# One core, attention and a gated convolution in one kernel: the list of 1,028 steps in a new sequence

## The chip, the cores and the metric

The kernel runs on one core of a Trainium2 chip. The metric is the device time of one execution in microseconds (us), lower is better; the time given for a kernel is the median of its runs. One core has five engines that take their own instruction queues: PE (TensorE, the matmuls), DVE (VectorE), ACT (ScalarE), POOL (GpSimd) and SP (SyncE, which here only issues DMA transfers). They meet only at semaphores: an instruction waits until what it reads has been written and what it overwrites has been read.

## The reference

Four batches of eight attention heads over 768 positions, and behind them a projection, a circular convolution along the positions with a given filter, a product of three terms and a second projection:

```python
def _attn_ref(q, k, v, is_retrieval, n_sink, window):      # 4 x 8 heads x 768 x 64
    scores = scale * np.matmul(q, k.transpose(0, 1, 3, 2))
    stream_keep = causal & (is_sink | in_win)              # 4 sinks, window of 64
    mask = np.where(retr, full_mask, stream_mask)          # heads 0, 2 and 6 see all before them
    ...                                                    # softmax along the keys
    return np.matmul(a, v)

def _moe_ref(x, w_proj, filter_fft, w_out):                # x: 4 x 768 x 512
    proj = x @ w_proj
    x1, x2, x3 = proj[..., :D], proj[..., D:2 * D], proj[..., 2 * D:]
    X2 = np.fft.rfft(x2, n=S, axis=1)
    H = np.fft.rfft(filter_fft, n=S, axis=0)
    x2_conv = np.fft.irfft(X2 * H, n=S, axis=1)
    return (x1 * x2_conv * x3) @ w_out
```

Inputs and output are float32; the kernel computes in bfloat16 with float32 sums.

## The kernel before

The heads are taken in 16 pairs, n = 0 to 15; pair n belongs to batch b = n // 4. The work is cut into 1,028 named steps in its main part. Each is a small function, and the program is two strings of names that `run` goes through: `AHEAD` (start-up, not touched) and then `FAST`. No scheduler stands behind them: the sequence of the names is the sequence of the instructions on each engine's queue. So a step earlier in the string is earlier on its engine, and the engines run against each other as their waits allow.

```python
def run(words):
    for word in words.split():
        name, _, slot = word.partition("@")     # @n: the PSUM bank from which the step's tile begins
        name, _, eng = name.partition("/")      # /v: DVE, /s: ACT, /p: POOL
        now.update(slot=slot, engine=eng)
        ops[name]()
```

A name without a letter has a fixed engine. A copying step (`ev`, L969) goes to DVE (L971), POOL (L973) or ACT (L975); a step of two operands (`two`, L978) to DVE or POOL. The eight PSUM banks are the tile `space`.

The steps of a pair n:

- `lq`, `lk`, `lv`: load q, k, v (SP, DMA). `cq`, `ck`, `cv`: cast them to bfloat16 (L971, L973 or L975).
- `T`: turn q and k, for n below 8 on PE with `E` taking them out of PSUM, from 8 on as a DMA transpose issued by SP.
- `kx`, `ks`, `vx`, `vs`: copies of keys and values that the windowed heads need.
- `sc n.c`: scores (PE, L1452), `sb` (PE, L1465, n below 4) adds the mask, `ex` the exponential (ACT, L1471) into `f_pT`; `mk`, `mr` (L978) multiply by a mask for n from 4 on.
- `at`: probabilities by values (PE, L1516), `rec` (DVE, L1522) the reciprocals of the sums, `nm` the division into `f_attn`: one DVE instruction (L1533), or, with /s, twelve ACT instructions (L1530).
- `fd`, `fe`, `fA`, `fS`, `fb` (L978) and `fr` (DVE): sums and differences ahead of the forward transform, `W` the transform itself (PE), `We` its copy into `f_xh`.
- `tn`, `te`: the attention's result turned, into `f_xT` (for n up to 7 and 15 on PE, else as a DMA transpose).

The steps of a batch b:

- `X b.t.u`: the projection x2 in the frequency domain (PE, L1620), t one of three parts of the spectrum; `Xe` copies it into `f_X`; `sw` swaps halves of part 2 by DMA; `pa`, `pb`, `pc` (L978) multiply by the filter `f_HAB` into `r_P`.
- `x1 b.cb.s`, `x3 b.cb.s`: the projections x1 and x3 (PE, L1655) of one fourth of the channels, cb; `xs` copies x1; `g` (DVE, L1674, and L1678 for cb = 3) multiplies by x3 into `r_gy`.
- `c b.cb.r`: the inverse transform (PE, L1685) from `r_P`, `ce` its copy, `cv b.cb.half` (DVE, L1696) into `f_conv`; `y` (L978) multiplies by `f_conv`. For cb = 3, `y` comes ahead of `g`: `y` multiplies `f_conv` by x1 and `g` then by x3; else `g` comes first.
- `o b.i.part`: the output projection (PE, L1712) from `r_gy`; `oe` copies it out of PSUM, `st` stores it (SP, DMA).

Once only: `lw part.half` (POOL, L1244) loads w_proj in six pieces into `f_wproj`, part 0 for x1, 1 for x2, 2 for x3; `lwo` w_out, `lfilt` the filter; `fold`, `F` and `H` (L1272 on DVE, L1274 on ACT) make `f_HAB` of the filter, with `Hd0`, `Hd1` as DMAs; `G`, `Gt`, `Ge`, `Gk` make the transforms' tables; `blank` steps are matmuls on zeros.

The PE's dependence on the others at the places that the change touches: in the new list `X2.0.0` uses the banks that `nm12` reads; in the old one `x12.1.1` comes behind `X2.0.0` and uses banks that `g1.3` reads; `c2.0.0` needs all three of `pc2.0`, `pc2.1` and `pc2.2`; `tn7` needs `nm7`.

Of the kernel before, what the change touches and what calls it, by code (L numbers as in the profile page):

```python
# [146 lines left out]
ex7.0 X0.1.0@2 rec5 mk6.1/p nm5/v X0.1.1 Xe0.0/s mk7.0/v sc7.1@0 fd5/v Xe0.1/s sc6.2@4 fe5/v X0.2.0@6 pa0.0/v
ex7.1 pb0.1/v X0.2.1 ck8/v ex6.2 x30.1.0@2 pa0.1/v Xe0.2/s fA5/v sc7.2@0 ck10/v W4.1@4 cq8/s x30.1.1 mk7.1/v
sw0.0 sw0.1 mr6/v ex7.2 sc6.4@6 W4.0 T8 mk6.2/v ck9/s g0.1 mk7.2/p tn5@0 tn4@1 cq10/s te5/v x30.2.1@2 te4/v
cv7/s T10 x30.2.0 fS5/v pc0.1/v We4/s x10.2.0@0 fb5/v vs7/v ex6.4 x10.2.1 pa0.2/v lq11 cq9/s vx7/v at6.0@4 fr5  # L150
cv8/s T9 pb0.2/v at6.1 xs0.2/s W5.1@6 W5.0 pc0.2/v We5/s lv11 g0.2 pb0.0/p c0.0.0@0 cv9/s c0.1.0@1 lk13 rec6
# [1681 lines left out]
```

## Time and profile before

| | |
|---|---|
| runs | 195.18, 195.27, 194.32 us, median 195.18 |
| profiled execution | 194.51 us, of it the span of the instructions 192.7 |
| granted TensorE clock | 0.997 |
| PE busy | 177.3 us (92%), 1688 matmuls |
| DVE busy | 166.4 us (86%), 322 instructions |
| ACT busy | 141.4 us (73%), 202 instructions |
| POOL busy | 74.2 us (39%), 106 instructions |
| DMA | 34.25 MB, mean 178 GB/s |

The profile names instructions by their line, engine, operation and tiles (out<-in). A row of the groups gives busy us, mean ns of one, the engine's idle time ahead of them and what ended it. A row of the timeline gives start and duration in us, and in brackets how long the engine had waited and for what. Since many steps share a line (L978 above all), a single step is told by its tiles and its place in time.

### The profile page before, as it was taken

What the parts mean: (1) busy time and instruction counts of PE and PEld (TensorE: products, weight loads), DVE (VectorE), ACT (ScalarE), POOL (GpSimd) and SP (SyncE); (2) the same over time, 40 slices, a digit from 0 to 9 for tenths busy, and PEclk for the clock granted to TensorE, in tenths of its full rate; (3) what the DMA queues carried; (4) which work ended last, traced back from release to release, by engine and by line L of the source; (5) the groups of instructions that cost most, each with busy time, mean ns of one, the idle gap of its engine ahead of it and who ended that gap; (6) DMA issues with size and microseconds to landing.
All of it is one profiled execution on the core that took longest, in us unless ns stands there. A gap on an engine that the chain in (4) does not pass through costs nothing.

```text
span 192.7 us, 4452 instructions
## 1 busy us (share of the span) xinstructions
PE 177.3 (92%) x1688; PEld 102.5 (53%) x1688; DVE 166.4 (86%) x322; ACT 141.4 (73%) x202; POOL 74.2 (39%) x106
## 2 busy tenths in 40 slices
...
GB/s 161 324 268 301 199 197 242 270 297 222 189 217 198 235 198 182 227 221 209 232 165 218 271 251 207 164 58 41 0 155 109 43 110 0 26 31 23 273 263 112
DMA packets 79759, 34.25 MB, mean 178 GB/s; under 512 B 69106, under 2 KB 76018, under 8 KB 79730
## 3 DMA queue, kind: packets, MB, share of 16 engines
...
## 4 chain that ended last, share of the span: by engine, by line
PE 41%; DVE 27%; DMA 16%; ACT 8%; issue 4%; SPq 1%; POOL 0%; DVEq 0%
PE space L1655 14%; DMA f_wproj<-in_moe_w_proj_dram 11%; PE space L1712 10%; PE space L1685 5%; DVE r_P L978 4%; PE space L1620 4%; DMA r_qk_f<-in_q_dram 3%; ACT f_pT L1471 3%; PE space L1452 3%; DVE f_pT L978 3%; PE space L1516 3%; DVE f_attn L1533 2%; DVE f_conv L1696 2%; DVE f_m L978 2%; ACT f_qkT L975 2%
## 5 line engine op out<-in xcount | busy, mean ns | idle before, releaser
L1471 ACT ACTIVATE f_pT<-space 128x1024 bf16<-128x1024 f32 (+3 forms) x68 | 60.3, 934 | 7.3 <-PE space L1452 4.0
L1655 PE MATMUL space<-f_xT,f_wproj 128*128 128x384 bf16 x256 | 47.9, 326 | 2.7 <-DVE r_gy L1678 1.7
L1655 PEld LDWEIGHTS <-f_wproj 128*128 128x128 bf16 x256 | 23.8, 98 | 19.7 <-issue 4.0
L1712 PE MATMUL space<-f_wout,r_gy 128*128 128x512 bf16 x96 | 24.0, 379 | 0.0
L1452 PE MATMUL space<-f_qkT 64*128 64x128 bf16 (+3 forms) x248 | 23.0, 251 | 0.7 <-DVE f_attn L1533 0.3
L1620 PE MATMUL space<-f_wproj,f_xh 128*128 128x512 bf16 x96 | 22.9, 379 | 0.4 <-ACT f_xh L975 0.3
L1685 PE MATMUL space<-f_Gi,r_P 128*128 128x384 bf16 x96 | 19.3, 327 | 1.8 <-DVE r_P L978 1.3
L978 POOL TENSOR_TENSOR f_fo<-f_attn 128x384 bf16<-128x384 bf16 x13 | 12.5, 967 | 20.5 <-DVE f_attn L1533 17.8
L978 DVE TENSOR_TENSOR f_pT<-f_pT,r_mtab 128x1024 bf16<-128x1024 bf16 (+3 forms) x33 | 19.4, 604 | 1.0 <-ACT f_pT L1471 0.9
L1452 PEld LDWEIGHTS <-f_qkT 64*128 64x128 bf16 x248 | 10.7, 94 | 15.0 <-issue 12.3
L1516 PE MATMUL space<-f_v_aug,f_pT 128*128 128x65 bf16 x392 | 17.7, 193 | 0.8 <-ACT f_pT L1471 0.5
L1516 PEld LDWEIGHTS <-f_pT 128*128 128x128 bf16 x472 | 16.6, 97 | 3.5 <-issue 0.6
L1696 DVE TENSOR_TENSOR f_conv<-f_evs,space 128x384 bf16<-128x384 f32 x32 | 16.3, 546 | 0.7 <-PE space L1685 0.2
L975 ACT COPY f_o<-space 128x1024 f32<-128x1024 f32 (+1 forms) x11 | 9.4, 859 | 8.4 <-PE space L1712 8.4
L1533 DVE TENSOR_TENSOR f_attn<-space,f_rec 128x768 bf16<-128x768 f32 x15 | 14.4, 957 | 0.5
L1620 PEld LDWEIGHTS <-f_xh 128*128 128x128 bf16 x96 | 8.8, 97 | 10.3 <-issue 0.7
L978 POOL TENSOR_TENSOR f_uv<-f_fo 128x256 bf16<-128x256 bf16 x15 | 11.4, 772 | 6.5 <-DVE f_fo L978 5.0
L1712 PEld LDWEIGHTS <-r_gy 128*128 128x128 bf16 x96 | 8.8, 98 | 9.1 <-issue 0.4
L978 POOL TENSOR_TENSOR f_pT<-f_pT,r_mtab 128x512 bf16<-128x512 bf16 (+1 forms) x6 | 8.3, 1379 | 13.2 <-ACT f_pT L1471 13.2
L975 ACT CAST f_xh<-space 128x768 bf16<-128x768 f32 x14 | 11.5, 820 | 2.4 <-PE space L1573 2.4
L1685 PEld LDWEIGHTS <-r_P 128*128 128x128 bf16 x96 | 8.5, 97 | 8.6 <-DVE r_P L978 2.2
L975 ACT CAST f_X<-space 128x1024 bf16<-128x1024 f32 x7 | 7.1, 1011 | 7.2 <-PE space L1620 7.2
(137 smaller groups left out, 346.6 us busy)
## 6 DMA issues: line engine op xcount, KB each, us to landing
...
r_qk_f<-in_k_dram SPq DMA_DIRECT2D x4, 384.0 KB, 11.1
...
```

Source lines behind the costliest of these rows:

```text
L975: nc.scalar.copy(out=out, in_=in_)
L978: (nc.gpsimd if now["engine"] == "p" else nc.vector).tensor_tensor(out, a, b, op)
L1452: nc.tensor.matmul(sc[:, bank, col:col + 128 * cnt], lhsT=keys, rhs=qkT(n)[rows, 0, 128 * i:128 * (i + cnt)], start=(col == 0 or not biase ...
L1471: nc.scalar.activation(out=pT(n)[:, c, :, 0:w], in_=held[f"sc.{n}.{c}"][:, :, 0:w], func=AF.Exp, scale=SCALE)
L1516: nc.tensor.matmul(att[:, hh, 65 * i:65 * i + 65], lhsT=pT(n)[:, c, bank, col:col + 128], rhs=values, start=(z == 0), stop=(z == len(here) ...
L1533: nc.vector.tensor_mul(attn(n).rearrange("p i hh d -> p hh i d"), rows[:, :, :, 0:64], held[f"rec.{n}"][:, :, :, None].to_broadcast([128, ...
L1620: nc.tensor.matmul(ps[:, u, :], lhsT=xh(b)[:, cc, chain, 128 * part:128 * part + 128], rhs=wproj()[:, cc, DM:2 * DM], start=(cc == 0), sto ...
L1655: nc.tensor.matmul(ps[:, s, 0:HS], lhsT=wproj()[:, cc, part * DM + cb * 128:part * DM + (cb + 1) * 128], rhs=xT(b)[:, cc, s * HS:s * HS + HS],
L1685: nc.tensor.matmul(ps[:, 0, 0:HS], lhsT=P(b)[:, t, u, ch], rhs=Gi()[:, tile_no], start=(m == 0), stop=(m == 2))
L1696: fn(conv[:, half * HS:half * HS + HS], held[f"evs.{b}.{cb}"], held[f"c_ps.{b}.{cb}.1"][:, 0, 0:HS])
L1712: nc.tensor.matmul(ps, lhsT=gy(b)[:, cb, i * 128:(i + 1) * 128], rhs=wout()[:, cb, :], start=(cb == 0), stop=(cb == NC - 1))
```

## The change

Only the string `FAST` is another; functions and `AHEAD` stay. It holds the same steps, each once. They stand in a new sequence, 136 of them have another engine letter, and the PSUM banks differ accordingly. Among the moves that the prediction speaks of: `H1.0`, `H2.0`, `H2.1`, `Ge1`, `Ge2` and `Gk1` from DVE to ACT; `nm12` from DVE to ACT; `y1.0` and `y1.1` from DVE to POOL, `pa2.1` from POOL to DVE; the six `lw` in another order; `mk14.0` behind c2.0.0; `lq14`, `T14` and `lk7` later on SP. `g1.3` stands behind the first half of `X2.2` instead of both; `X2.0.0` stands behind `x12.0` and `x32.0.0`. The diff, cut to the lines that hold these:

```diff
@@ -124,72 +124,72 @@
 """
 
 FAST = """
-blank12@0 lq2 lk2 blank10@1 xp0 lv1 G31/p ck0/v blank11@2 mtab2 parb lk3 T0.1@3 lv0 cq0/s blank8@4 G32/v
-blank2@5 skew1/s skew0/p lk4 E0.1/s blank5@6 lq4 G30/v T0.0@7 kz2 Gm01 G00/s lv3 kz0 blank6@0 ck1/v cq1/s mtab3
-lq3 T1.1@1 blank9@2 lv2 E0.0/s Gm00 T1.0@4 kz1 Gm1 blank1@5 lk6 btab G01/p blank7@6 E1.0/v lq6 ck2/p sc0.0@2 lk7
-sb0.0 sc0.2@6 cq2/v ex0.0 T2.1@0 alt Gk1/v lq5 T2.0@5 E1.1/v lk5 sb0.2 cv1/p Gt0@4 ex0.2 lq7 sc0.1@2 sb0.1 Gk0/v
-blank4@1 lv4 Ge0/v ck3/p E2.0/s sc0.4@6 sb0.4 ks1/s kx1/v ex0.1 E2.1/v lfilt sc1.0@4 T3.1@1 ex0.4 sb1.0 Gm2
-lw2.0 Gt2@0 ex1.0 kx2/v sc1.1@2 cv0/p sc0.3@6 sb0.3 sb1.1 ex0.3 ck4/v ones1 Gt1@4 lv6 lwo Ge2/v ks2/s ex1.1
-sc1.2@6 Ge1/v sb1.2 ones0 lw1.0 sc2.3@4 ex1.2 cq4/v sc0.5@2 lw1.1 sb0.5 E3.1/v blank3@0 ex0.5 T4.1@6 lw2.1
-at0.1@2 vx1/v ks3/p vs1/v T4.0@7 lw0.1 cq3/s sc2.1@0 kx3/v lw0.0 E4.1/v at0.0 E4.0/s ones2 ex2.3 cv3/v T3.0@7
...
-ex2.0 fold1/v sb2.2 sc3.2@4 tn1@7 ex2.2 fd0/p sc3.0@2 sb3.0 te1/s fe1/v sb3.2 te0/v fA0/p ex3.0 F1.1@0 fd1/v
-fold0/v sc2.4@6 H1.1/s F2.1@2 H1.2/s fA1/v fS0/v F1.0@1 ex2.4 fb0/v fS1/v ex3.2 fr1 F2.0 H1.0/v F0.0@0 cv2/p
-F0.1@6 H2.0/v H0.0/s lv5 vx2/p sc3.1@4 fb1/p sb3.1 H0.1/s H2.1/v Hd0 vs2/p H0.2/s sc4.0@0 ck6/p ex3.1 at2.0@6
...
-fd2/p lk10 T7.1@2 te3/v W1.1 fd3/v x30.0.1@4 We1/s fS3/v fA2/p x10.3.0@6 cq5/v sc4.3@0 fA3/p x10.3.1 ck5/s fS2/v
...
-We2/s sc5.1@0 rec4 mk5.2/p W3.0@6 nm4/v W3.1 ex5.1 sc5.0@4 H2.5 sc6.3@2 We3/s mk5.1/v sc6.0@0 ex5.0 fe4/p
...
-x30.3.0@6 mk8.1/p rec7 kx10/s cv0.3.0 ce0.2/s x30.3.1 cv0.3.1 nm7/s mk8.2/v sc10.3@0 y0.3/v at8.0@4 g0.3 at8.1
-ks9/v y0.0/v ex10.3 tn7@6 fe7/p rec8 sc10.1@2 te7/v c0.2.1@7 ex10.1 fd7/v x11.3.1@0 fA7/p cv0.2.0 cv11/s x11.3.0
...
-x31.0.0 mk9.1/v lq14 ex9.2 W6.0@0 g1.0 W6.1 cq12/s sc9.0@2 o0.1.0@6 fA8/v mk10.0/v We6/s T12 fr7 o0.0.0 mk9.2/v
...
-T14 W8.1@0 pc1.1/v Xe1.0/s W8.0 at10.1@2 mk11.2/v at10.0 We8/s pa1.0/v x31.2.1@4 ex12.4 rec10 cv13/p nm10/v
...
-c1.2.0@2 fr11 ce1.0/s fb11/v c1.0.1@3 mk12.2/v ce1.1/s W11.1@0 cv1.0.0 ck15/s W11.0 c1.1.1@5 cv1.0.1 We11/s
-c1.3.0@4 T15 mk12.0/v vs13/v c1.3.1@3 ce1.2/s cv1.1.0 X2.1.1@0 cv1.1.1 y1.0/v ce1.3/s X2.1.0 ks14/p kx14/v
-y1.1/v X2.2.1@4 cv1.3.0 Xe2.1/s cv1.3.1 c1.2.1@2 y1.3/v X2.2.0 pa2.1/p g1.3 X2.0.0@0 Xe2.2/s cv1.2.1 cv1.2.0
-x12.1.1@6 sw2.1 y1.2/v at12.0@4 sw2.0 mk13.0/v at12.1 kx15/s mk13.2/v ks15/s sc13.1@2 cv15/s rec12 X2.0.1 nm12/v
-ex13.1 vs15/p x12.1.0 tn12 pb2.1/v Xe2.0/s x12.0.1@4 mk13.1/v x12.0.0 xs2.1/s pa2.2/v sc14.0@2 pb2.2/v xs2.0/s
-sc14.3@0 vx15/v o1.3.0@6 vx14/v ex14.3 pc2.2/v x32.0.0@4 pb2.0/v ex14.0 x32.0.1 fe12/v pc2.1/v x12.3.1@0
-mk14.0/p g2.0 c2.0.0@2 x12.3.0 ce2.0/s fd12/v pa2.0/v o1.3.1 xs2.3/s o1.2.0 pc2.0/v o1.2.1 at13.1@4 fS12/v
...
-x13.3.1 g3.1 x13.2.0@4 xs3.3/s x13.2.1 pb3.2/v o2.0.0@2 pc3.2/v xs3.2/s o2.0.1 pb3.0/v x33.2.1@6 c3.0.0@4
...
-o3.0.0@4 oe3.3/v o3.0.1 o3.1.0@5 st3.3 oe3.0/s o3.1.1 st3.0 oe3.1/s st3.1
...
+blank10@4 G32/s lv1 blank8@5 E0.1/s cq0/v lq3 Gk0/p ck1/s T0.0@6 Gm01 lv3 blank6@7 G01/p E0.0/s Gm1 T1.1@0 alt
+lk4 Gm00 ones2 Gk1/s G30/p lv2 sc0.1@4 cq1/s G00/v sb0.1 kz0 blank5@1 Gm2 cq2/s E1.1/v lk6 sc0.3@2 sc0.4@6 lq6
+ck2/p T1.0@1 ex0.1 Gh0 sb0.4 sb0.3 Gh1 T2.0@0 E1.0/v kz2 lk5 ex0.3 T2.1@4 lq5 E2.0/v Gt2@5 E2.1/s lk7 cv0/p
+sc0.0@2 ex0.4 sc0.2@0 kx2/v ks1/p Gt0@4 lv6 kx1/p ks2/s Ge0/v Ge2/s ck3/p Gt1@6 lq7 blank2@7 Ge1/s sb0.2 cq4/v
+blank11@4 lfilt ex0.2 sc1.2@4 sb1.2 sc2.3@6 ex1.2 cv1/v sc0.5@0 sb0.5 lw0.0 lv4 ex0.5 sc1.0@4 cq3/v sb0.0 T3.1@0
+ex0.0 lw0.1 T3.0@1 E3.1/v sb1.0 ones0 lw2.1 E3.0/s at0.1@2 ones1 ex1.0 vs1/v at0.0 vx1/p kx3/v sc1.1@0 ex2.3
+rec0 lw1.1 sb1.1 nm0/v ck4/p sc2.1@4 cv3/s sb2.1 T4.0@6 ks3/v ex1.1 fd0/p tn0@7 T4.1@2 vx3/v ex2.1 fe0/p at1.0@0
+at1.1 vs3/v E4.1/s te0/v fS0/p sc3.1@4 sb3.1 rec1 E4.0/v lw2.0 blank9@3 ex3.1 lwo sc3.0@2 nm1/v sb3.0 lw1.0
...
+F0.0@4 fA1/v fr1 H0.1/s sc2.2@0 fb1/p sb2.2 H0.0/s F1.0@5 cv2/v H0.2/v lv5 ex2.2 F2.1@2 vx2/p vs2/v fA0/v F2.0
+H1.0/s te1/v fb0/p at2.1@0 fr0 H2.0/s at2.0 ck6/p sc4.0@6 rec2 Hd0 at3.1@4 nm2/v ex4.0 at3.0 lk9 rec3 H2.1/s
...
+fS2/p te2/v blank12@2 mk4.0/v H1.1/s x10.3.0@2 fb3/v We0/v cq6/s x10.3.1 fA2/v lq9 x30.0.1@6 xs0.3/s ck7/v cq5/v
+kx6/s lk10 T7.1@0 fr2 x10.0.1@4 E7.1/s mk4.1/v fb2/v T5.0@2 H1.2/s x10.0.0 cv6/v ck5/s ks7/p W3.0@0 kx7/v vs6/p
...
+We2/v T6.0@5 lq10 E5.0/s kx5/p E6.0/v at4.0@0 ks5/s lv7 cv5/s sc5.2@2 H2.3 sc5.1@4 H2.4 ex5.2 at4.1 lv8 vx5/p
...
+te6/v mk8.2/p nm7/s x30.3.0@0 cv0.3.0 x30.3.1 mk8.1/v y0.3/v at8.0@6 fd6/v g0.3 at8.1 fS6/p ks10/s tn7@2 fe7/p
...
+st0.3 sc11.2@6 mk11.0/v Xe1.1/s X1.0.0@0 lq14 fr9 ex11.2 at10.1@4 pa1.1/v W8.0@2 ck15/s W8.1 mk11.2/v at10.0
...
+cv1.0.0 y1.1/p X2.1.1@0 cv1.0.1 T14 ce1.2/s X2.1.0 vs13/v y1.0/p ce1.3/v at12.0@4 Xe2.1/s cv1.3.0 at12.1 cv1.3.1
+x12.0.1@0 cv15/s y1.3/v rec12 X2.2.0@6 pa2.1/v nm12/s g1.3 vx15/p X2.2.1 ks15/p pb2.1/v x12.0.0 vs15/v pc2.1/v
+x32.0.0@2 Xe2.2/s tn12 ks14/p X2.0.0@4 mk13.0/v xs2.0/s fd12/v c1.2.1@6 kx15/v sw2.1 mk13.2/v kx14/s x32.0.1
+sw2.0 cv1.2.1 x12.3.0@0 cv1.2.0 pa2.2/v x12.3.1 y1.2/v X2.0.1 xs2.3/s g2.0 x12.1.1@6 Xe2.0/s pb2.2/v sc13.1@0
+sc14.3@2 pc2.2/v ex13.1 sc14.0@4 x12.1.0 pb2.0/v ex14.3 o1.2.0@0 mk13.1/v xs2.1/s o1.2.1 pa2.0/v c2.0.0@2 ex14.0
...
+sc14.2@4 fr12 sc15.2@0 rec13 mk14.0/p ex14.2 c2.0.1@2 nm13/v c2.1.1@3 ex15.2 mk14.2/p sc15.0@4 cv2.1.1 tn13
...
+st2.1 c3.0.0@4 pc3.0/v x13.3.0 ce3.0/s g3.2 c3.0.1@5 xs3.3/s c3.1.0@2 cv3.0.0 c3.1.1@3 cv3.0.1 ce3.1/s c3.2.0@4
...
+o3.1.1 st3.2 oe3.1/s st3.1
...
```

More of the change, by code (lines that the diff above doesn't have):

```diff
@@ L147 @@
[L147 to L151, printed above, removed]
```

78 lines of the change are left out of this document (43 added, 35 removed).

## The prediction

> **What bounds the kernel now.** I read the page's first lines, then the windows of 10 us, then the chain that ended last, and last the timeline at the places where the chain leaves the PE.
>
> ```profile
> span 192.7 us, 4452 instructions
> PE 177.3 (92%) x1688; PEld 102.5 (53%) x1688; DVE 166.4 (86%) x322; ACT 141.4 (73%) x202; POOL 74.2 (39%) x106
> PE 41%; DVE 27%; DMA 16%; ACT 8%; issue 4%; SPq 1%; POOL 0%; DVEq 0%
> ...
> 10.00:20.00 10.00, 9.09 (x100) 5.09 (x100) 9.77 (x15) 7.91 (x12) 8.09 (x13) 1.00 1.18 278
> 20.00:30.00 10.00, 9.27 (x151) 6.63 (x152) 8.63 (x16) 8.80 (x12) 6.77 (x11) 1.00 1.21 197
> 30.00:40.00 10.00, 9.45 (x115) 5.51 (x114) 9.56 (x18) 9.10 (x14) 4.74 (x7) 1.00 1.16 266
> 40.00:50.00 10.00, 8.97 (x82) 5.29 (x81) 7.91 (x15) 9.40 (x15) 6.25 (x8) 1.00 1.15 245
> 50.00:60.00 10.00, 9.52 (x135) 6.09 (x134) 8.40 (x18) 9.94 (x14) 6.54 (x8) 1.00 1.12 208
> 90.00:100.00 10.00, 10.00 (x88) 5.65 (x86) 9.07 (x20) 7.15 (x11) 2.63 (x3) 1.00 1.26 210
> 120.00:130.00 10.00, 8.30 (x85) 4.79 (x84) 9.67 (x16) 5.05 (x8) 2.73 (x2) 1.00 0.49 119
> 130.00:140.00 10.00, 8.86 (x85) 4.93 (x84) 9.47 (x18) 6.55 (x9) 1.86 (x2) 1.00 0.09 20
> 140.00:150.00 10.00, 10.00 (x117) 6.20 (x112) 9.50 (x20) 7.22 (x10) 3.83 (x3) 1.00 0.57 127
> ```
>
> The window columns are stretch, length, then busy us of PE, weight load, DVE, ACT and POOL. The matmul work is the same before and after, so the PE's waits are what a new order can change. By the chain's shares (third row) PE, DVE and DMA, in this order, carry it to its end. There are three kinds of stretch. From 10 to 60 us no engine is full: the PE loses 0.5 to 1.0 in each window and ACT loses less and less, until it is full at 50. From 140 on the PE is full and nothing but its own work counts. Between them, at 120 to 140, the PE loses 1.70 and 1.14 while DVE is busy and ACT is not. The timeline names the waits (the three longest that it shows on the PE after the start), and beside them the engines that caused them:
>
> ```profile
> 43.55 0.81 PE L1655 MATMUL space<-f_xT,f_wproj 128*128 128x384 bf16 x4 [0.78 <-DMA f_wproj<-in_moe_w_proj_dram]
> 125.70 0.81 PE L1655 MATMUL space<-f_xT,f_wproj 128*128 128x384 bf16 x4 [1.70 <-DVE r_gy L1678]
> 135.65 0.66 PE L1685 MATMUL space<-f_Gi,r_P 128*128 128x384 bf16 x3 [1.15 <-DVE r_P L978]
> ...
> 122.12 2.12 POOL L978 TENSOR_TENSOR r_P<-f_X,f_HAB 128x1024 bf16<-128x1024 bf16 x1 [3.21 <-ACT f_X L975]
> 122.28 2.38 DVE L978 TENSOR_TENSOR f_conv<-f_conv,f_x1s 128x768 bf16<-128x768 bf16 x1
> 133.86 1.19 POOL L978 TENSOR_TENSOR f_pT<-f_pT,r_mtab 128x512 bf16<-128x512 bf16 x1 [4.52 <-ACT f_pT L1471]
> 133.95 1.64 DVE L978 TENSOR_TENSOR r_P<-r_P,f_m 128x1024 bf16<-128x1024 bf16 x1
> ```
>
> The op y1.3 (122.28) took 2.38 where ten ops of its size take 0.62 each (the r_gy row below): it began 0.16 behind a POOL op of 2.12 and ended 0.42 behind that op's end. The op g1.3 follows it, and the PE waits 1.70 for g1.3. The second wait is the same thing again: pc2.1 (133.95) began 0.09 behind mk14.0 on POOL.
>
> **The change, part by part.** No instruction is added or removed. 136 words change their engine, and nearly all change place. I price it by what stands ahead of a step on an engine, in rows of one op of each kind. The rows:
>
> ```profile
> L1274 ACT ACTIVATE f_HAB<-space 128x1024 bf16<-128x1024 f32 x1 | 1.0, 1024 | 0.8 <-PE space L1265 0.8
> L1274 ACT ACTIVATE f_HAB<-space 128x512 bf16<-128x512 f32 x4 | 2.2, 596 | 0.0
> L975 ACT COPY f_xT<-space 128x768 bf16<-128x768 bf16 x1 | 0.8, 799 | 0.0
> L975 ACT CAST f_v_aug<-f_v_f 128x768 bf16<-128x768 f32 x7 | 6.2, 882 | 3.2 <-PE space L1516 3.2
> L975 ACT COPY f_kx<-f_qkT 128x256 bf16<-128x256 bf16 x2 | 0.8, 411 | 0.0
> L1530 ACT ACTIVATE f_attn<-space,f_rec 128x64 bf16<-128x64 f32 x12 | 2.6, 346 | 0.0
> L1272 DVE TENSOR_SCALAR f_HAB<-space 64x1024 bf16<-64x1024 f32 x2 | 2.4, 1217 | 0.0
> L971 DVE CAST r_x1s<-space 128x768 bf16<-128x768 f32 x1 | 1.0, 952 | 0.0
> L971 DVE COPY f_o<-space 128x1024 f32<-128x1024 f32 x2 | 2.4, 1218 | 0.8 <-PE space L1712 0.8
> L971 DVE COPY f_Gi<-space 128x768 bf16<-128x768 bf16 x3 | 1.7, 556 | 0.0
> L978 DVE TENSOR_TENSOR r_gy<-f_conv,r_gy 128x768 bf16<-128x768 bf16 x10 | 6.2, 620 | 0.2
> L1533 DVE TENSOR_TENSOR f_attn<-space,f_rec 128x768 bf16<-128x768 f32 x15 | 14.4, 957 | 0.5
> L978 POOL TENSOR_TENSOR r_gy<-f_conv,r_gy 128x768 bf16<-128x768 bf16 x2 | 3.6, 1783 | 16.2 <-DVE f_conv L1696 16.2
> ```
>
> *First part, up to nm7 (80 us): ACT.* Ahead of nm7, which the PE's tn7 waits for, ACT gains H1.0, H2.0 and H2.1 (3 x 1.02 = 3.06), Ge1 and Ge2 (as the f_xT row, 2 x 0.80 = 1.60), Gk1 (0.41) and one value cast more (cv3 and cv5 on, cv6 off: 0.88). It loses one E more than it gains (0.80), H0.2 (0.60), We2 (0.82) and kx7, ks1 and ks6 (0.8 together). The other swaps cancel. Net +2.9 us. Against that stands the idle time of ACT in the windows from 10 to 50: 2.09 + 1.20 + 0.90 + 0.60 = 4.79. The new list gives ACT its first ready work sooner: sc0.1, sc0.3 and sc0.4 stand on the PE ahead of the first exponential's turn, where the old list had one score and a wait of 1.31 (row below), and H and Ge work lies where ACT waited for scores. If none of the idle is filled, the stretch ends 2.9 later; if all of it, 1.9 sooner. I take three quarters (3.6), because ACT's list is now the longer one all through the stretch, so it has something ready when a score is late: -0.7. DVE in turn has 1.3 less ahead of g0.3, so it doesn't take over.
>
> ```profile
> 12.14 1.02 ACT L1471 ACTIVATE f_pT<-space 128x1024 bf16<-128x1024 f32 x1 [1.31 <-PE space L1465]
> 22.70 20.71 DMA f_wproj<-in_moe_w_proj_dram
> L1244 POOL DMA_DIRECT2D f_wproj<-in_moe_w_proj_dram x6: 612/622/722, 16.4 to 22.7; - x6
> DMA to landing us min/median/max: 11.0/16.6/20.7
> ...
> 25.80 0.91 POOL L978 TENSOR_TENSOR f_fo<-f_attn 128x384 bf16<-128x384 bf16 x1 [0.53 <-DVE f_attn L1533]
> ```
>
> *The weights.* POOL issued lw2.0, lw1.0, lw1.1, lw2.1, lw0.1, lw0.0; now lw0.0, lw0.1, lw2.1, lw1.1, lw2.0, lw1.0. The first landed at 16.4 + 11.0 = 27.4 and the last at 22.7 + 20.7 = 43.4, so one lands every 3.2 us. The PE's first use needs lw0 and lw2, so it needed the sixth piece and now needs the fifth, at 27.4 + 4 x 3.2 = 40.2 (an estimate from these rows). The 0.78 at 43.55 then goes, but what is late next at that place is ACT, so I count it inside the -0.7 and not again. lw2.0 is now queued on POOL behind vx1, ck4, fd0, fe0 and fS0, and fd0 waits for nm0, which ended by 25.8 (row): a rival below.
>
> *Second part, 119 to 136 us: DVE.* Ahead of g1.3, DVE loses H1.0, H2.0, H2.1 (3.65), xs1.2 and xs1.3 (1.90), oe0.3 (1.22), y1.0 and y1.1 (1.24), Ge1 and Ge2 (1.11): 9.1. Moves the other way are four E on and three off (0.95), We2 (0.95), three more casts of q and k (1.7) and two more of v (1.1), H0.2 (0.75), pa2.1 (0.69), and small ones for -0.8: 5.3. Net -3.8. The step that waits for g1.3 also stands 1.2 us of PE work later in the list, so DVE is 5.0 us better placed there; the same count for pc2 and c2.0.0 gives 6.1. The waits were 1.70 + 1.15 = 2.85, so I take all: -2.85 (bounds 0 and -3.6, which adds the smaller losses of the same two windows).
>
> Does POOL take it back? pa2.1 (2.1 on POOL) goes to DVE and mk14.0 comes later, but y1.1 and y1.0 (1.78 each) come to POOL just before y1.3. By the rows at 122 and 134 the price is at most one POOL op for each DVE op that falls behind it, 2 x 1.78 = 3.6, less than the 5.0 of relief: 0. The Trainium skill speaks here (SBUF — State Buffer, Who interferes with whom): a DVE op with two SBUF inputs and a GpSimd op that reads SBUF exclude each other for the whole instruction, whichever comes first. The rows at 122.12 and 122.28 agree. By that rule the two y ops give back up to 3.6 of waiting, which is the second rival.
>
> *nm12 on ACT.* It was one DVE op (0.96) and is now 12 ACT instructions, 2.6 together (the nm7 row). X2.0.0 reuses its PSUM banks. Between at12 and X2.0.0 the PE now has x12.0, X2.2 and one half of x32.0: 3 x 0.65 + 8 x 0.216 = 3.7 (paces from the rows of the tail: 1.30/8 and 5.19/24). rec12 (last row below) and nm12 take 0.23 + 2.6 = 2.8 of it. The cover is 0.9; if rec12 falls behind a held y1.3 it is gone, and up to 0.9 is lost. I take +0.2. Behind nm12 on ACT stand Xe2.2 and so the swap sw2, pb2.2 and pc2.2; c2.0.0 comes 1.7 us of PE work later than X2's last part is done and more besides, so they are covered.
>
> ```profile
> 180.08 1.30 PE space L1655 x8
> 181.38 5.19 PE space L1712 x24
> ```
>
> ```profile
> L1522 DVE RECIPROCAL f_rec<-space 128x12 f32<-128x12 f32 x16 | 3.6, 227 | 0.4 <-PE space L1516 0.3
> ```
>
> *SP and the rest.* lq14 and T14 go behind lv15, st0.3 and T15; T14 was issued some 17 us before its first use, so 4 us less is nothing. lk7 goes behind lk5 and lq5 (two issues of 1.5) while its user T7.1 goes 2 us of PE work later: 0 to +1.1. The last 50 us are PE work back to back; the new list has one place there with little cover (c3.0 behind the swap sw3), as the old one had. The tail is the same: o3.1, oe3.1 on ACT, its store. Together +0.4 (bounds 0 and +1.5).
>
> *Sum:* -0.7 - 2.85 + 0.2 + 0.4 = -2.95 us. The profiled execution took 194.51 us and would take 191.6. It lies 0.67 under the median of the runs shown, 195.18, within their 194.32 to 195.27, so the forecast for the median is 195.18 - 2.95 = **192.2 us**.
>
> **The rivals.**
>
> *ACT cannot absorb it (slower).* Place: ACT's queue from 10 to 130 us. Its list grows by 2.9 ahead of nm7 and by 2.6 with nm12. If its idle time lies where the new words can't go (waits for loads and for the PE), both come out at the PE. Price with none absorbed: 195.2 - 2.85 + 2.9 + 2.6 + 0.4 = 198.2. It decides from the point where less than about 3 of these 5.5 us are absorbed. For it: ACT is at 9.94 of 10 already at 50. Against it: 4.79 idle before, 2.85 at 90 to 100 and 4.95 at 120 to 130. Chance 0.18.
>
> *POOL holds DVE again (no change).* The two y ops on POOL and their readers keep the PE waiting 2.85 as before; then 195.2 - 0.7 + 0.6 = 195.1. For it: both of the old waits came about so. Against it: 5.0 of relief. Chance 0.14.
>
> *Late weights (slower).* lw2.0 is issued behind fS0, by the rows above at 25.8 plus two fd/fe and one fS, 2.5, so at 28.3 at the latest; with the longest landing, 20.7, it lands at 49.0, 5.4 later than now. 195.2 + 5.4 - 2.85 + 0.6 = 198.4. It decides from a landing at about 46. Against it: the long landings are a queue behind earlier pieces, and there are fewer waiting now. Chance 0.06.
>
> *More than I count.* All of ACT's idle is filled (-1.9) and all 3.6 of the second part go: 195.2 - 1.9 - 3.6 + 0.6 = 190.3. Chance 0.16.
>
> **How the numbers follow.** Forecast 0.46, the rivals 0.18, 0.14, 0.06 and 0.16. A measurement of this kernel can tell about 0.5% from no change, 0.98 us: 194.2 to 196.2. The forecast's own range is 190.9 to 193.8, all faster; more than I count is faster; POOL lies within, but a third of it would be faster. Slower is ACT and the weights, of which a little lies within: faster 0.65, same 0.13, slower 0.22. The range reaches from 190.0, a little below the best case, to 197.5, where an eighth of ACT's 5.5 us is absorbed (198.2 - 0.7); it leaves out the far parts of the ACT and weights cases.
>
> **What would show it.** Right: no PE wait over 1 us between 119 and 137 in PE time, ACT's idle time from 10 to 50 us under 2, no wait for the weights, the first step of the third batch's X at 117 or earlier, the last o step ending near 183.6. Wrong: a PE wait for ACT's nm12 or Xe2.2, y1.3 or pc2 at over 1.5 us behind a POOL op with the PE waiting, PE waits for exponentials between 50 and 83 that sum to over 2 us more than now, or a wait for f_wproj over 1 us.

## The result, and the profile after

The new list takes 192.00 us (median of 6 runs, 191.41 to 192.99), the old one 194.77 (6 runs): ratio 0.9853, 95% interval 0.9807 to 0.9899, that is 2.8 us less. Medians and ranges here and below hold all runs; ratios leave out the executions that took over 1.5% longer than the fastest of their kernel. The forecast was 192.2 of 195.18. The sum came out; two of its terms did not, in opposite directions. The profiled execution of the new list is its slowest run, 192.99, and so shows half of the gain only, 1.5 us against the 194.51 of the profile before. I look for the parts in it first and then ask other executions which of them are always there.

The page of the new list, its first lines and its chain, and the stretches of 10 us (columns as before):

```profile
span 191.3 us, 4463 instructions
PE 175.1 (92%) x1669; PEld 102.5 (54%) x1688; DVE 154.5 (81%) x318; ACT 149.1 (78%) x217; POOL 73.9 (39%) x106
PE 59%; ACT 10%; DMA 9%; SPq 7%; DVE 5%; issue 5%; POOL 1%; ACTq 0%; DVEq 0%; POOLq 0%
...
10.00:20.00 10.00, 9.25 (x106) 5.49 (x104) 6.70 (x12) 9.73 (x15) 8.23 (x16) 1.00 1.20 272
20.00:30.00 10.00, 8.04 (x143) 5.50 (x143) 6.24 (x15) 8.20 (x10) 5.31 (x8) 1.00 1.20 209
30.00:40.00 10.00, 8.40 (x100) 4.64 (x98) 7.40 (x17) 8.48 (x11) 4.57 (x6) 1.00 1.16 272
40.00:50.00 10.00, 9.35 (x78) 5.82 (x78) 7.85 (x19) 9.83 (x15) 4.33 (x7) 1.00 1.10 242
120.00:130.00 10.00, 9.89 (x88) 5.79 (x89) 9.58 (x21) 7.80 (x20) 5.50 (x5) 1.00 0.70 153
130.00:140.00 10.00, 9.95 (x107) 5.86 (x106) 9.24 (x18) 8.72 (x11) 3.78 (x4) 1.00 0.25 77
```

The rows are the profiled execution's. In the chain DVE has gone from 27% to 5%, and SP's queue has come in with 7%. From 120 to 140 the PE is idle for 0.16 where it lost 2.84. From 20 to 40 it is the other way round: it loses 3.56 where it lost 1.28. PE's count is 1669 of 1688 matmuls: 19 records are missing from this trace, and a missing record reads as idle time. I therefore use lateness: the start of a matmul less the work that stands ahead of it in the list, where each matmul counts with the median spacing of its line and shape in the old list's trace (169.2 us for the whole list). It needs no missing record, and compares lists of different order at equal work. Here it is for the profiled executions of the kernels that follow, in us:

| work done, us | old | new | new_again | new_then_old | old_pa_mk_on_dve | new_h_ge_on_dve | new_weights_behind_vx1 |
|---|---|---|---|---|---|---|---|
| 15 | 3.47 | 4.66 | 4.64 | 4.63 | 3.37 | 4.27 | 4.64 |
| 35 | 7.14 | 10.02 | 8.62 | 8.05 | 6.94 | 12.59 | 7.86 |
| 80 | 13.33 | 14.96 | 13.56 | 14.23 | 12.69 | 17.62 | 12.80 |
| 105 | 13.61 | 15.41 | 13.76 | 14.51 | 12.96 | 17.83 | 13.00 |
| 165 | 17.19 | 15.58 | 13.93 | 18.08 | 14.23 | 18.05 | 13.17 |
| from 105 to 165 | 3.58 | 0.17 | 0.17 | 3.57 | 1.27 | 0.22 | 0.17 |

Up to 80 us of work the new list loses 1.6 to the old one in its profiled execution, and from 105 to 165 it wins 3.4. Of the 1.6, 1.2 are there at 15 us of work already, and that much (4.63 to 4.66 against 3.47) in every profile of a kernel with the new list's whole first part unchanged. The PE's waits from 10 to 20 us in the new list, where ACT is now busy for 9.73 of the 10 us (7.91 before):

```profile
PE space L1227 <- ACT f_pT L1471: 0.3, 1, 0.3
PE space L1452 <- ACT f_pT L1471: 0.2, 1, 0.2
PE space L1452 <- ACT f_qkT L975: 0.2, 1, 0.2
PE space L1407 <- ACT f_pT L1471: 0.2, 1, 0.2
```

All four are for ACT; the old list has two there, 0.5 for a cast on POOL and 0.2 for ACT. The timeline of the new list at the place of the second gain:

```profile
120.38 3.42 POOL L978 TENSOR_TENSOR r_gy<-f_conv,r_gy 128x768 bf16<-128x768 bf16 x2 [5.78 <-DVE f_conv L1696]
120.56 1.01 DVE L1696 TENSOR_TENSOR f_conv<-f_evs,space 128x384 bf16<-128x384 f32 x2
121.48 0.80 DVE L971 COPY f_v_x<-f_v_aug 64x520 bf16<-64x520 bf16 x1
123.94 0.56 DVE L978 TENSOR_TENSOR f_conv<-f_conv,f_x1s 128x768 bf16<-128x768 bf16 x1
124.56 0.63 DVE L978 TENSOR_TENSOR r_P<-f_X,f_HAB 128x1024 bf16<-128x1024 bf16 x1
124.79 2.57 ACT L1530 ACTIVATE f_attn<-space,f_rec 128x64 bf16<-128x64 f32 x12
125.10 0.94 DVE L1678 TENSOR_TENSOR r_gy<-f_conv,space 128x768 bf16<-128x768 bf16 x1
126.56 0.28 DVE L971 COPY f_v_x<-f_v_aug 64x520 bf16<-64x520 bf16 x1
127.52 0.81 PE L1620 MATMUL space<-f_wproj,f_xh 128*128 128x512 bf16 x3
```

y1.3 (123.94) takes 0.56 instead of 2.38, because the two y steps on POOL have just ended (120.38 + 3.42 = 123.80) and pa2.1 (124.56) follows it on DVE. And the place of its largest waits in the first part:

```profile
24.41 0.82 POOL L973 CAST f_qk_bf<-f_qk_f 128x768 bf16<-128x768 f32 x1 [4.29 <-DMA f_qk_f<-in_k_dram]
25.29 0.51 PE L1407 MATMUL space<-r_identity,f_qk_bf 128*128 128x128 bf16 x6 [1.64 <-POOL f_qk_bf L973]
34.32 0.56 DVE L971 CAST f_v_aug<-f_v_f 128x768 bf16<-128x768 f32 x1 [2.46 <-DMA f_v_f<-in_v_dram]
34.95 0.27 PE L1516 MATMUL space<-f_v_aug,f_pT 128*128 128x65 bf16 x3 [0.44 <-DVE f_v_aug L971]
35.67 0.20 PE L1516 MATMUL space<-f_v_x,f_pT 128*128 128x65 bf16 x1 [0.46 <-DVE f_v_x L971]
```

The PE waits 1.64 for T4.1, behind the cast ck4 and that behind the load lk4, and 0.9 in at2.1, behind cv2 and the load lv2. Both are loads that SP issues beside the first big transfers of POOL. The answers on the tiles `f_wproj` (new) and `f_v_f` (the old list's line, then the new list's) say how long such a transfer takes:

```profile
L1244 POOL DMA_DIRECT2D f_wproj<-in_moe_w_proj_dram x6: 612/622/857, 16.2 to 29.1; - x6
DMA to landing us min/median/max: 8.2/13.4/14.5
...
DMA to landing us min/median/max: 3.2/4.9/15.4
...
DMA to landing us min/median/max: 3.9/5.3/17.3
```

A half of v lands 5.3 after its issue at the median and 17.3 at worst; the worst is the second half of lv2, in both lists. It is not alone: the loads of q and k that SP issued from 16 to 30 us took 14.9 to 18.0 us to land in the new list and 15.3 to 17.2 in the old one.

### The profile page after: what moved, and what is told of

It is laid out like the page before. It is cut to its first block, busy times and chain, and to the rows that moved or that the text cites. A ratio compares the mean times of both kernels' runs of the same rounds, so it can differ in the third digit from the quotient of the medians.

```text
span 191.3 us, 4463 instructions
## 1 busy us (share of the span) xinstructions
PE 175.1 (92%) x1669; PEld 102.5 (54%) x1688; DVE 154.5 (81%) x318; ACT 149.1 (78%) x217; POOL 73.9 (39%) x106
## 4 chain that ended last, share of the span: by engine, by line
PE 59%; ACT 10%; DMA 9%; SPq 7%; DVE 5%; issue 5%; POOL 1%; ACTq 0%; DVEq 0%; POOLq 0%
PE space L1655 17%; PE space L1620 10%; PE space L1712 10%; DMA f_v_f<-in_v_dram 9%; PE space L1685 8%; PE space L1516 6%; ACT f_pT L1471 5%; PE space L1452 5%; SPq L1369 4%; SPq L1383 3%; ACT f_qkT L975 1%; PE space L1571 1%; PE space L1569 1%; DVE f_attn L1533 1%; POOL f_fo L978 1%
## 5 line engine op out<-in xcount | busy, mean ns | idle before, releaser
L1471 ACT ACTIVATE f_pT<-space 128x1024 bf16<-128x1024 f32 (+3 forms) x68 | 59.0, 923 | 4.6 <-PE space L1452 3.0
L1655 PE MATMUL space<-f_xT,f_wproj 128*128 128x384 bf16 x256 | 48.4, 326 | 0.3
L1655 PEld LDWEIGHTS <-f_wproj 128*128 128x128 bf16 x256 | 23.6, 98 | 16.7 <-issue 1.5
L1712 PE MATMUL space<-f_wout,r_gy 128*128 128x512 bf16 x89 | 23.3, 379 | 0.4 <-issue 0.2
L1452 PE MATMUL space<-f_qkT 64*128 64x128 bf16 (+3 forms) x248 | 21.7, 250 | 1.5 <-ACT f_Hn L1274 0.5
L1452 PEld LDWEIGHTS <-f_qkT 64*128 64x128 bf16 x248 | 10.6, 94 | 14.9 <-issue 12.9
L978 DVE TENSOR_TENSOR f_pT<-f_pT,r_mtab 128x1024 bf16<-128x1024 bf16 (+3 forms) x32 | 17.4, 566 | 0.3 <-ACT f_pT L1471 0.3
L1696 DVE TENSOR_TENSOR f_conv<-f_evs,space 128x384 bf16<-128x384 f32 x32 | 16.2, 547 | 1.6 <-PE space L1685 1.1
L978 POOL TENSOR_TENSOR f_uv<-f_fo 128x256 bf16<-128x256 bf16 x11 | 9.7, 880 | 17.9 <-DVE f_fo L978 12.5
L978 POOL TENSOR_TENSOR f_br<-f_fo,f_uv 128x256 bf16<-128x256 bf16 x10 | 8.0, 804 | 18.4 <-DVE f_uv L978 17.9
L1533 DVE TENSOR_TENSOR f_attn<-space,f_rec 128x768 bf16<-128x768 f32 x14 | 13.4, 955 | 0.4
L975 ACT CAST f_xh<-space 128x768 bf16<-128x768 f32 x13 | 10.4, 810 | 3.8 <-PE space L1573 3.8
L1407 PE MATMUL space<-r_identity,f_qk_bf 128*128 128x128 bf16 x96 | 7.7, 219 | 2.6 <-POOL f_qk_bf L973 1.6
L978 POOL TENSOR_TENSOR f_fo<-f_attn 128x384 bf16<-128x384 bf16 x10 | 9.2, 928 | 1.5 <-DVE f_attn L1533 0.9
```

The source lines that it names most:

```text
L975: nc.scalar.copy(out=out, in_=in_)
L978: (nc.gpsimd if now["engine"] == "p" else nc.vector).tensor_tensor(out, a, b, op)
L1407: nc.tensor.transpose(ps[:, 0, t * 128:(t + 1) * 128], qk_bf(n)[:, a, t].rearrange("p hh d -> p (hh d)"), identity())
L1452: nc.tensor.matmul(sc[:, bank, col:col + 128 * cnt], lhsT=keys, rhs=qkT(n)[rows, 0, 128 * i:128 * (i + cnt)], start=(col == 0 or not biase ...
L1471: nc.scalar.activation(out=pT(n)[:, c, :, 0:w], in_=held[f"sc.{n}.{c}"][:, :, 0:w], func=AF.Exp, scale=SCALE)
L1533: nc.vector.tensor_mul(attn(n).rearrange("p i hh d -> p hh i d"), rows[:, :, :, 0:64], held[f"rec.{n}"][:, :, :, None].to_broadcast([128, ...
```

## The experiments

The old list ran beside each of them; its medians in three sets of runs were 195.19, 194.27 and 194.57.

**Which part gives what.** Around 70 us the two lists have done the same steps but one, so each can be continued by the other.

```diff
 old_then_new:  old words 1 to 416 (... pb0.2/v at6.1 xs0.2/s), then the rest in the new order
 new_then_old:  new words 1 to 415 (... x30.2.0 pb0.2/v te4/s), then the rest in the old order
+               W5.1@0   (was W5.1@6 in the old list)
```

> The old list up to xs0.2 (416 words, about 70 us), then the new list's words in the new list's order. Theory: in the two traces the PE of the new list is 1.7 us behind at this place and gains 3.4 us between 119 and 137, two changes that have nothing to do with each other. Then this kernel has only the gain: 194.8 - 3.4 = 191.4, or 192.0 - 1.7 = 190.3 counted from the other end: 190.3 to 191.4, faster than both lists. Rival 1, the prediction's split (first part -0.7, second -2.85): 191.9 to 192.7, not faster than the new list. Rival 2, the two are tied (the waits at 119 to 137 are gone because the PE comes there 1.7 us later and DVE has caught up): part of the waits comes back, 192.5 to 194.

> The new list up to te4 (415 words, about 70 us), then the old list's words in the old list's order (W5 in another PSUM bank). Theory: only the loss of the first part: 194.8 + 1.7 = 196.5, with the waits of 1.70 and 1.15 at 120 to 137 as before. Rival 1, the prediction's split: 194.8 - 0.7 = 194.1. Rival 2, tied: the waits shrink because the PE comes later, 195.0 to 195.5.

Measured: old_then_new 191.56 (191.13 to 194.15), ratio 0.9836 (0.9770 to 0.9902). new_then_old 196.48 (195.22 to 197.38), ratio 1.0072 (1.0036 to 1.0108). The second part of the new list alone gives the whole gain; its first part alone costs 1.4 us (0.7 to 2.1). The prediction's split (first part -0.7) is refuted. The rival that ties the two together falls too: in new_then_old the PE comes to 105 us of work 0.9 later than in the old list, and the waits are there as before, 1.69 and 1.15:

```profile
123.02 2.12 POOL L978 TENSOR_TENSOR r_P<-f_X,f_HAB 128x1024 bf16<-128x1024 bf16 x1 [3.41 <-ACT f_X L975]
123.19 2.37 DVE L978 TENSOR_TENSOR f_conv<-f_conv,f_x1s 128x768 bf16<-128x768 bf16 x1
126.60 0.81 PE L1655 MATMUL space<-f_xT,f_wproj 128*128 128x384 bf16 x4 [1.69 <-DVE r_gy L1678]
134.75 1.19 POOL L978 TENSOR_TENSOR f_pT<-f_pT,r_mtab 128x512 bf16<-128x512 bf16 x1 [4.52 <-ACT f_pT L1471]
134.85 1.64 DVE L978 TENSOR_TENSOR r_P<-r_P,f_m 128x1024 bf16<-128x1024 bf16 x1
136.55 0.66 PE L1685 MATMUL space<-f_Gi,r_P 128*128 128x384 bf16 x3 [1.15 <-DVE r_P L978]
```

What did not come: old_then_new should have been 0.6 to 1.7 below the new list and is 0.4 below it, which the intervals can't tell from nothing. Its profiled execution, 194.15, is 2.6 over its median, with a wait of 2.3 at 53 to 56, and is not used for the first part.

**Is it the POOL ops that hold DVE?** Two letters of the old list:

```diff
-... y1.3/v X2.2.0 pa2.1/p g1.3 ... pc2.1/v x12.3.1@0 mk14.0/p g2.0 c2.0.0@2 ...
+... y1.3/v X2.2.0 pa2.1/v g1.3 ... pc2.1/v x12.3.1@0 mk14.0/v g2.0 c2.0.0@2 ...
```

> The old list with two letters changed: pa2.1 and mk14.0 on DVE instead of POOL. Theory (a DVE op that falls behind a running POOL op is held): y1.3 and pc2.1 take 0.6 to 0.7 each, DVE has 0.63 and 0.42 more to do, and of the PE's waits of 1.70 and 1.15 about 1.8 in all goes: 193.0. Rival (DVE is simply too far behind there, and the POOL ops only happen to lie beside it): DVE is 0.6 to 1.0 longer, the waits stay or grow, 194.8 to 195.8.

Measured: 192.03 (191.44 to 195.51), ratio 0.9867 (0.9797 to 0.9938), that is 2.6 us less (1.2 to 4.0), so the 1.8 us expected lie within. Its timeline:

```profile
121.62 0.56 DVE L978 TENSOR_TENSOR f_conv<-f_conv,f_x1s 128x768 bf16<-128x768 bf16 x1
122.10 0.68 DVE L978 TENSOR_TENSOR r_P<-f_X,f_HAB 128x1024 bf16<-128x1024 bf16 x1
123.70 0.81 PE L1655 MATMUL space<-f_xT,f_wproj 128*128 128x384 bf16 x4 [0.35 <-DVE r_gy L1678]
131.96 0.68 DVE L978 TENSOR_TENSOR r_P<-r_P,f_m 128x1024 bf16<-128x1024 bf16 x1
132.70 0.66 PE L1685 MATMUL space<-f_Gi,r_P 128*128 128x384 bf16 x3 [0.20 <-DVE r_P L978]
```

With more work on DVE, y1.3 takes 0.56 and pc2.1 0.68, and the waits fall from 1.70 and 1.15 to 0.35 and 0.20. So DVE was not too slow there; it was held. By lateness this gives 3.58 - 1.27 = 2.3, which is what the two waits lost (1.35 and 0.95); another 0.6 in its profile came before 80 us, and 191.44 was the fastest of its runs. Two letters give what no measurement here can tell from the whole new list.

**The two other moves at that place**, the y steps back on DVE and nm12 back on DVE, each in the new list:

> The new list with y1.0 and y1.1 on DVE instead of POOL: POOL has 3.4 us less between 120 and 124, DVE about 1.2 more ahead of y1.3 and g1.3. Theory (what counted there was pa2.1 on POOL just ahead of y1.3, which is on DVE in the new list): g1.3 comes 1.2 later and the PE, which did not wait there at all, waits for 0 to 1.2: 192.0 to 193.2. Rival (the move of the y steps was a part of the gain): 193.5 or more. Rival (POOL's y steps hold DVE up): faster, 191.0 to 191.6.

```diff
-cv1.0.0 y1.1/p X2.1.1@0 cv1.0.1 T14 ce1.2/s X2.1.0 vs13/v y1.0/p ce1.3/v ...
+cv1.0.0 y1.1/v X2.1.1@0 cv1.0.1 T14 ce1.2/s X2.1.0 vs13/v y1.0/v ce1.3/v ...
```

Measured: 192.08 (191.92 to 192.89), ratio 0.9875 (0.9820 to 0.9929), the same as the new list. From 105 to 165 its PE falls behind by 0.35 instead of 0.17. The move of the y steps to POOL gave nothing and took nothing back that these runs can tell.

> The new list with nm12 on DVE (one op of 0.96) instead of ACT (twelve, 2.6 together). In the new list's profile nm12 ends at 127.3 and X2.0.0 begins at 127.5 without a wait, so the prediction's +0.2 was not there: taking it back wins nothing. g1.3 comes 0.96 later, to the very time at which x32.0.0 needs its bank: 192.0 to 192.4. Rival (ACT is relieved by 2.6 and Xe2.2, the swap and c2.0.0 come earlier): 191.4 or less.

```diff
-... pa2.1/v nm12/s g1.3 ...
+... pa2.1/v nm12/v g1.3 ...
```

Measured: 191.81 (191.40 to 192.90), ratio 0.9901 (0.9867 to 0.9935), not told apart from the new list. The PE goes from 13.56 to 14.21 late between 105 and 165, so nm12 on ACT is worth 0 to 0.5 as it stands, not a loss of 0.2.

**What costs time in the first part?** First the load lk4 earlier on SP:

```diff
-lq4 ... lv1 ... lq3 ... lv3 ... lk4
+lq4 ... lk4 lv1 ... lq3 ... lv3
```

> The new list with one word moved: lk4 ahead of lv1 on SP (it stood behind lv1, lq3 and lv3, and landed at 24.4 instead of 16.9, behind the first weights). Theory: the PE's wait of 1.64 for ck4 ahead of T4.1 goes and nothing is late in its place: 192.0 - 1.6 = 190.4. Rival: the next late thing takes it back (lv2, which at2.1 waits for, or ACT, which has 2.9 us more to do ahead of nm7): -0.5 or less, 191.5 to 192.0, and the PE is still 1 us or more behind the old list at 60 us.

Measured: 195.44, but over a range of 191.62 to 197.78, with no ratio that could be given; the time decides nothing. Its profile does show where the wait went:

```profile
25.59 0.83 ACT L975 CAST f_v_aug<-f_v_f 128x768 bf16<-128x768 f32 x1 [3.13 <-DMA f_v_f<-in_v_dram]
27.40 0.25 PE L1516 MATMUL space<-f_v_aug,f_pT 128*128 128x65 bf16 x3 [3.43 <-ACT f_pT L1471]
```

lk4 is in time, and the second half of lv3, which now stands where lk4 stood, beside the first big transfer, is late. Its cast cv3 stands on ACT ahead of an exponential, and the PE waits 3.43 instead of 1.64. Neither the gain nor the small loss that I expected: by this profile the wait belongs to the place in the queue and not to the load.

Then the first four large transfers later on POOL, behind vx1:

```diff
-blank11@4 lfilt ex0.2 ... lw0.0 lv4 ... lw0.1 ... lw2.1 E3.0/s ... vx1/p kx3/v ...
+blank11@4 ex0.2 ... lv4 ... E3.0/s ... vx1/p lfilt lw0.0 lw0.1 lw2.1 kx3/v ...
```

> The new list with four words moved on POOL: lfilt, lw0.0, lw0.1 and lw2.1 stand behind vx1 (they were issued from 15.2 on, now from about 18.3 on). Theory: the load that SP issues next to the first of these large transfers is the one that comes late (lk4 at 24.4 in the new list, PE wait 1.64 ahead of T4.1; lv3 when lk4 stood earlier, wait 3.4; lv2 at 34.2, waits of 0.9 at at2.1). With lk4, and half of lv2, ahead of them, these waits go: 192.0 - 1.6 to 2.5 = 189.5 to 190.4. Rival 1: the filter lands 2 to 3 later, and fold0 and the F steps at 29 to 31 wait for it: 191 to 192.5. Rival 2: the large transfers are not the cause, and lk4 is late again: 192.

> The kernel with lfilt, lw0.0, lw0.1 and lw2.1 behind vx1 once more, beside the new list. Theory (lk4 and lv2 land in time: lk4 before 20 instead of 24.4, lv2 at 22.4 instead of 34.2): 0.8 to 2.4 below the new list of this call, 189.8 to 191.4. Rival: the waits come back in another place in most executions, and it is within 0.5 of the new list.

Measured: 191.71 (190.81 to 192.46), ratio 0.9862 (0.9805 to 0.9918), and the second time 192.25 (191.09 to 194.09), ratio 0.9899 (0.9857 to 0.9940), beside the new list itself at 192.06. No gain that can be told. In the first profile the two waits are gone and the PE is 0.5 ahead of the old list at 80 us; in the second one the filter came late:

```profile
30.74 0.96 DVE L978 TENSOR_TENSOR r_gy<-r_gy 128x1536 bf16<-128x1536 bf16 x1 [3.03 <-DMA r_gy<-in_moe_filter_fft_dram]
31.75 1.45 PE L1265 MATMUL space<-r_gy,r_G 128*128 128x512 bf16 x6 [2.19 <-DVE r_gy L978]
```

That is rival 1 of the expectation in one execution of two: the fold waits 3.03 for the filter, and F0.1 2.19 for the fold. lv2 has landed by 22.5 in both, 12 earlier than in the new list; the large transfers behind it pay for that.

Last, the new list itself once more:

> The new list unchanged, beside the three that follow and the old list on the same chip. Theory: 191.4 to 192.5, and in its profile the PE behind the old list's by 1 to 2 us at 60 us, with its largest wait ahead of T4.1 or at2.1 (the loads lk4 and lv2 behind the first large transfers). Rival: the loss in the first part was one execution's accident; then the PE is within 0.5 us of the old list there.

Measured: 192.06 (190.46 to 193.08), ratio 0.9886 (0.9835 to 0.9938). Its profiled execution, 191.48, is only 0.23 behind the old list at 80 us. Its waits of the PE from 20 to 42 us:

```profile
PE space L1452 <- ACT f_Hn L1274: 0.5, 1, 0.5
PE space L1516 <- DVE f_v_x L971: 0.5, 1, 0.5
...
PE space L1407 <- POOL f_qk_bf L973: 0.2, 1, 0.2
```

The wait for lk4 has shrunk from 1.64 to 0.2: its length is an accident of single executions, the wait at at2.1 is there again. The five profiles with the new list's unchanged first part stand 1.63 (new), 0.23 (new_again), 0.90 (new_then_old), 1.36 (new_y_on_dve) and -0.28 (new_nm12_dve) behind the old list's at 80 us of work. At 15 us of work they all stand 1.2 behind it (4.63 to 4.66 against 3.47; 3.31 to 3.77 in the four profiles that begin with the old list). From there to 80 us they take 8.4 to 10.3 beside the old list's 9.9. So the part of the loss that is always there comes before the PE waits for either of the loads lk4 and lv2, and the rest goes either way. ACT is full there in each of them, 14.7 of the 15 us from 5 to 20, where it was busy for 12.2 in the old list. That this is the cause is not shown: in new_again 0.8 of the 1.7 that the PE waits there in rows of 0.2 and more are for DVE, and no run takes the start apart.

**Was it ACT?** Six letters of the new list back:

```diff
-H1.0/s H2.0/s H2.1/s Ge1/s Ge2/s Gk1/s
+H1.0/v H2.0/v H2.1/v Ge1/v Ge2/v Gk1/v      (each in its place in the new list)
```

> The new list with six letters back to DVE: H1.0, H2.0, H2.1, Ge1, Ge2, Gk1. ACT has about 5.1 us less ahead of nm7, DVE about 5.3 more. Theory (loads bound the first part of the new list, not ACT): the PE is as far behind the old list at 60 us as with the new list, 1.3 to 1.9: 191.7 to 192.5. Rival (ACT's longer queue is the loss): the 1.3 to 1.9 comes back, 190.2 to 190.8, or, if DVE can't take it over, slower than 193.

Measured: 195.27 (194.54 to 196.90), ratio 1.0048 (1.0009 to 1.0087), 3.2 us above the new list's 192.06 of another set of runs. Of my three cases it is the last one, and not a close one. DVE's timeline there:

```profile
33.57 0.56 DVE L971 CAST f_v_aug<-f_v_f 128x768 bf16<-128x768 f32 x1 [2.41 <-DMA f_v_f<-in_v_dram]
34.98 1.21 DVE L1272 TENSOR_SCALAR f_HAB<-space 128x1024 bf16<-128x1024 f32 x1
37.32 1.21 DVE L1272 TENSOR_SCALAR f_HAB<-space 64x1024 bf16<-64x1024 f32 x1
39.83 1.23 DVE L1272 TENSOR_SCALAR f_HAB<-space 64x1024 bf16<-64x1024 f32 x1
41.09 0.96 DVE L1533 TENSOR_TENSOR f_attn<-space,f_rec 128x768 bf16<-128x768 f32 x1
```

cv2 holds DVE's queue for 2.41 until lv2 lands, and behind it stand nm2 and nm3, for which the PE waits. The three H steps among them push nm3 (41.09) by 3.65. On ACT they lay beside this. Two more things lie in this profile: the wait for lk4, 1.5, and a granted TensorE clock of 0.50 from 37.0 to 43.7 us, at which the PE's work takes longer (six matmuls of L1589 0.82 at 43.07, and 0.51 at 45.39 when the clock is back). Neither carries the loss alone: a run of this kernel with a granted clock of 0.992, like those of the new list (0.989 to 0.997), took 194.92, and the wait of 1.64 for lk4 was in the new list's 192.99 too. That the H steps do it, and not Ge or Gk1, is read from the timeline and was not tried by itself; at 15 us of work, with Ge1, Ge2 and Gk1 back on DVE, this kernel is 0.4 less late (4.27) than the new list.

Two other letters taken off ACT, on top of the moved transfers:

> The same with two letters more: E7.1 and H1.2 on DVE instead of ACT. In the profile with the weights moved, ACT is busy 4.90 to 5.00 of every 5 us from 40 to 80, and DVE is idle for 1.7 in 45 to 50. Theory (ACT bounds 40 to 80 once the loads are in time): 0.5 to 1.4 below the kernel with the weights moved, 189.0 to 190.5. Rival (DVE's steps behind E7.1 and H1.2 come later and the PE waits for them, as with the six letters): same or slower, 191 to 192.

```diff
-E7.1/s ... H1.2/s
+E7.1/v ... H1.2/v      (and the four words behind vx1, as above)
```

Measured: 192.73 (191.38 to 194.93), ratio 0.9915 (0.9878 to 0.9952): no gain, as the rival had it. So ACT, full from 40 to 80, is not shown to set the pace by itself.

**The order of the weights alone**, in the old list:

> The old list with the names of the six lw words in the order of the new one (lw0.0, lw0.1, lw2.1, lw1.1, lw2.0, lw1.0 at the old six places). The PE's first use then needs the fifth piece, landing at about 40, not the sixth at 43.4. The prediction's step: the wait of 0.78 at 43.55 goes and another takes most of it back: 194.0 to 195.2. Rival (the wait was worth its full length): 194.0 or less. Rival (no effect beyond the wait's place): 194.8 to 195.2, and the PE as far along at 60 us as in the old list.

```diff
-lw2.0 ... lw1.0 ... lw1.1 ... lw2.1 ... lw0.1 ... lw0.0
+lw0.0 ... lw0.1 ... lw2.1 ... lw1.1 ... lw2.0 ... lw1.0      (at the old list's places)
```

Measured: 196.04 (194.22 to 197.33), ratio 1.0079 (1.0041 to 1.0117), slower, which no theory had. In its profiled execution (194.26, its second fastest) the wait for `f_wproj` is gone and the PE is 0.1 earlier than in the old list at 80 us of work. Where the time goes in its other runs is open, and so whether this order costs the new list something too; the 1.2 that the new list is late at 15 us of work is no part of it: it is there at 9 us of work (3.88 against 2.69), which the new list reaches at 12.9 us, and the first weights are issued at 16.2.

## Why the prediction was right, and where it was not

*Second part: the waits went as forecast, but mostly not for the reason that I counted, and the gain was larger.* Forecast -2.85 with bounds 0 and -3.6; the lateness says 0.17 - 3.58 = -3.4. The PE waits for g1.3 and for pc2 are both gone, as said; but I counted DVE's relief, while old_pa_mk_on_dve shows that two POOL ops beside DVE were two thirds of it: 2.3 of 3.4 with no relief at all. The other 1.1 can be the relief; no run shows it by itself. The rival that POOL holds DVE again through the two y steps was wrong, and the rows say why. While they run (120.38 to 123.80), DVE has the L1696 steps, which read PSUM and SBUF and take 0.51 each as ever (546 ns in the group of 32 before). Of the copies between SBUF tiles one is held (121.48, 0.80, its like at 126.56 takes 0.28), and y1.3 comes behind both. The Trainium skill (SBUF — State Buffer, Who interferes with whom) says that a DVE instruction with at most one SBUF input does not contend, except in the modes that copies can enter; these rows agree.

*ACT: the step that failed.* I took -0.7, with three quarters of ACT's idle time filled and under 2 us of it left between 10 and 50. In the windows above 0.27 + 1.80 + 1.52 + 0.17 = 3.76 are left, in those of new_again and new_nm12_dve 2.5 and 2.0. So 1.0 to 2.8 of the 4.79 were filled and not 3.6, and the first part came out at -0.3 to +1.6 by five profiles, +1.4 by the times of new_then_old. The term that was mis-sized is this share. The mistake has three parts. Moving H, Ge and Gk1 to ACT is right, by 3.2 us, and, as the timeline has it, for a reason that I did not count: DVE's queue has no slack behind cv2. The loss that stays, 1.2, is there at 15 us of work: from 10 to 20 us, the window with the most idle time, ACT did fill up as I said (0.27 left of 2.09), and the PE came no sooner for it but waited for ACT and DVE in pieces of 0.2 to 0.5; I had taken every idle us that is filled for a us gained. And the loss that comes and goes is in the loads lk4 and lv2, of which lk4 was moved behind lv1, lq3 and lv3: in *SP and the rest* I followed lq14, T14 and lk7 and not it. The wait of 1.64 that this can cost lies a little over that step's bound of +1.5.

*The weights: right.* lw2.0 was issued at 27.7, by my bound at 28.3 at the latest, and the longest of the six took 14.5 us to land, not 20.7. The PE's first L1655 comes at 44.71 without a wait, so the rival of late weights was not there. What their order costs in the old list, 1.5 us by the ratio (0.8 to 2.3), I had not foreseen.

*nm12: no loss.* Its cover was 0.9 by my count. Its twelve instructions end at 124.79 + 2.57 = 127.36 and X2.0.0 begins at 127.52: the cover was 0.16, and just held.

*The marks that I gave.* No PE wait over 1 us from 119 to 137: so. ACT's idle time under 2: no, 3.76 (2.0 in new_nm12_dve at the least). No wait for `f_wproj`: so. The third batch's first X step at 117: no, 120.84 (119.19 in new_again). The last o step at 183.6: 184.95, and 183.30 in new_again. The sum as the profiles have it is about +0.8 (mean of the five) - 3.4 = -2.6, beside -2.8 measured and -2.95 forecast. The first part is 1.5 worse than I said; the second is 0.55 better, and the +0.6 for nm12, SP and the tail does not show beside these. That the errors nearly cancel is luck.
